# Longer stretches for the letters of a scheduling string: PIECE from 10000 to 16000, and a string made anew

## The chip, the cores and the metric

The kernel runs on one core of one Trainium2 chip. The metric is device time in microseconds (us) of one execution, and less is better. Each kernel is executed several times. The kernel before takes 689.98 us (median of 3 runs, 689.96 to 690.01).

## What is computed

There are 2048 tokens with 640 features. They are normalised (layernorm without weights). Two branches read the result `xn`, and the output is the input plus both of them. The first is attention with 32 query heads of 20 features that share one key head and one value head. The second is a feed-forward network 640 -> 1728 -> 640 with silu between.

```python
xn = layernorm(x)                                  # 2048 x 640
q = (xn @ wq) in 32 heads of 20;  k = xn @ wk;  v = xn @ wv
p = softmax(q @ k^T / sqrt(20))                    # 32 x 2048 x 2048
attn = (p @ v, heads side by side) @ wo
ffn = silu(xn @ w1) @ w2
out = x + attn + ffn
```

The softmax needs 32 x 2048 x 2048, some 134 million, exponentials, and these set the scale of the kernel.

## The kernel before, in words

**Tiling.** Queries are cut into 4 blocks of 512, heads into 8 groups of 4, keys into 16 tiles of 128. A *head tile* is one head, one key tile and one query block: a matmul with 32 contracted rows (L1078) that writes 128 x 512 scores into one PSUM bank. Four heads lie in the four row groups of TensorE's array, so up to four such matmuls run side by side. There are 4 x 8 x 16 x 4 = 2048 head tiles, in 32 groups (a query block and four heads) of 64.

**Two ways to an exponential.** The first is ScalarE (ACT): `make_s_act` (L1126) issues an operation named S for two or three head tiles into neighbouring banks, and one ACTIVATE with Exp (L1166) turns 128 x 1024 or 128 x 1536 scores into bf16. The second is an approximation in integer arithmetic: VectorE (DVE) adds a bias to one head tile and writes int16 (L1409, `p1`). When the four heads of a key tile are there, two copies with other shifts are made, one on GpSimd (POOL, L1448) and one on DVE or POOL (L1453, L1448), and the sum of the three, weighted, stands for the exponential. `dve_items` claims key tiles for this way, from the end of a group.

**Products with the values.** For each key tile of a group, four matmuls of 32 columns (L1201) add exp(scores) times v into one bank, U: one pass (PV) for a tile of ACT, three passes (PVd) for a tile of DVE, one for each shifted copy. At the end of a group U is copied out, divided by the sums (a POOL multiplication, L860, after a round of small DMAs) and packed for the output product.

**Other work of TensorE (PE).** Beside these come jobs: the query projections (`q`), the hidden layer (`h`, tanh on ACT at L773), the output tiles of the first three query blocks (`out`), and for the last block `y`: eight half tiles (128 x 320), each a chain of 14 to 17 passes at L447. A few of these passes are cut in row groups (L454, `row`) and laid beside a set of S matmuls that leaves a row group free. At the very end, for the last group alone, stand `sum` (L999), `spread` (L1017) and `fin` (L447): they divide by the last group's sums on PE, and add its product with wo to the y tiles. DVE then evicts five banks (L967) and the last stores go out.

**What sets the order.** All of this is one program that `build` works out in Python before anything runs. It keeps a clock for each engine with costs written into the file, and commits one operation after another. On PE, `step_pe` (L1842) collects candidates of the kinds S, PV, PVd, DVE head tile, row slice and job, and takes the first ready one in an order of preference. When nothing is ready and the gap it reckons is over 250 ns (120 ns after a pass of 32-column matmuls), it may put in a `fill`, a matmul on zeros (L1725). How it prefers is governed by some thirty parameters (BASE, L105): how far ahead of ACT an S may be, how long a job may hold back an S, how many batches may be open, and so on. A letter of the string PLAN names a small set of replacements for these (RULES, L106). Letter n holds while the planner's PE clock lies between n x PIECE and (n+1) x PIECE nanoseconds; behind the string's end the letter is `a`, which replaces nothing.

```python
while not finished():
    if sc.t["pe"] >= piece * PIECE:
        ru.__dict__.update(BASE)
        ru.__dict__.update(RULES[rule(piece)])
        piece += 1
```

Each engine then executes its own list strictly in that order. Waits between engines are semaphores that `emit` derives from what each operation reads and writes. So the string decides nothing but the order of the five lists and which operations share an instruction: how many head tiles one Exp takes, whether a shifted copy is on DVE or POOL, where fills stand, how many passes are cut in rows. The number of head tiles on ACT and on DVE can change too, since key tiles are claimed as the planner goes.

Of the kernel before, what the change touches and what calls it, by code (L numbers as in the profile page):

```python
# [81 lines left out]
POOL_J = (2,)  # L82
SWITCH = {"s": 97.0, "p": 98.0, "f": 98.0}
SPRIO = 0.5
PIECE = 10000.0
STEPS = 1
YC = (0, 0, 3, 3)
EARLY = 1
# [17 lines left out]
RULES = dict(a={}, b=dict(keep=0.0), c=dict(lagp=3), d=dict(lagp=5), e=dict(lagp=0), f=dict(patience=200.0), g=dict(dwant=0.0),  # L106
             h=dict(zcap=4), i=dict(zcap=3), j=dict(homes=0), k=dict(leadmax=-1.0, lead=-1.0), l=dict(lead=0.08, leadmax=0.1),
             m=dict(need=740.0), n=dict(hold=0.0), o=dict(stay=640.0), p=dict(open=1), q=dict(slack=560.0), r=dict(hungry=1000.0), s=dict(claim=9), t=dict(open=3), u=dict(claim=4), v=dict(want=2), w=dict(slack=850.0), x=dict(hold2=4), y=dict(bnd=0), z=dict(pj=-1e9), A=dict(rows=0), B=dict(rows=2, rowmin=2), C=dict(pj=2000.0), D=dict(openlag=3), E=dict(pj=8000.0), F=dict(hold2=3), G=dict(rows=1), H=dict(half=0), I=dict(half=3), J=dict(stay=560.0), K=dict(stay=720.0), P=dict(need=560.0), Q=dict(hold=120.0), L=dict(uopen=3), M=dict(uopen=4), N=dict(uopen=5), O=dict(uopen=0))
PLAN = "acbgxnoQpQJvpnaQodtxzpvEoQJBJoaodpJqQaDqJovpkBrnvxBxQJBfaaooHoatano"


def rule(n):
    return PLAN[n] if n < len(PLAN) else "a"
PACE = 1.0
# [214 lines left out]
def build(nc, A_x, A_wq, A_wk, A_wv, A_wo, B_x, B_w1, B_w2, out, stack):  # L329
# [1648 lines left out]
    def finished():  # L1978
        return (att["pgroup"] >= NGR and not pro and not misc and not misc_front and cur_job[0] is None
                and all(not sc.pools[e] for e in sc.ENG))  # L1980
# [3 lines left out]
# [3 lines that stand above are left out]
# [187 lines left out]
```

## Time and profile before

| what | value |
|---|---|
| median of 3 runs | 689.98 us |
| the profiled execution, whole | 690.16 us |
| its span, first to last instruction | 688.3 us |
| what lies around the span | 1.9 us |
| VectorE (DVE) busy | 591.3 us, 86% of the span |
| GpSimd (POOL) busy | 581.7 us, 85% |
| granted TensorE clock | 1.00 throughout |

The profile is one execution as the hardware recorded it. An engine is busy while at least one instruction of its own runs. Instructions of one engine overlap: the next begins before the last has left the pipeline. So the mean duration of an instruction is longer than the time by which it holds up its successor, and where a sum is wanted one takes the distance between starts. The ends of matmuls are modelled. "Idle before" is the time in which an engine ran nothing, and the releaser is the instruction whose end let it go on. The chain is followed back from the last instruction: at each step to what released it, or to the instruction before it on its engine.

### The profile page before, as it was taken

Reading aid. Unit: us, or ns where it says so; the run is one execution under the profiler, and the core shown is the slowest. Engines: PE = TensorE matmul, PEld = TensorE weight load, DVE = VectorE, ACT = ScalarE, POOL = GpSimd, SP = SyncE. Lnnn points to the kernel's source line nnn. Section 1 sums busy time; section 2 is a strip of 40 time slices with the busy share of each in tenths; the row PEclk is TensorE's granted clock in tenths of the full one; section 3 lists DMA queues with packets and bytes.
Section 4 is the critical chain, followed back from the end, with each engine's and each line's share of the span. In section 5 each row is a group of like instructions: output and inputs, shape, how many; then the busy total and the mean of one; then the engine's idle time right before and its main releaser. Section 6 shows DMA issues by size and latency. Waiting matters only on the chain.

```text
span 688.3 us, 22511 instructions
## 1 busy us (share of the span) xinstructions
PE 675.7 (98%) x9821; PEld 232.2 (34%) x9821; DVE 591.3 (86%) x1017; ACT 666.4 (97%) x728; POOL 581.7 (85%) x349
## 2 busy tenths in 40 slices
PE   8999999999999999999999999999999999999998
PEld 6432222222333333322323333332233333333345
DVE  7899988999989878798898897889999898987953
ACT  6999999999999999999999999999999999999992
POOL 6658899898988998899898889888889987879990
PEclk9999999999999999999999999999999999999999
DMA  8643220222221222422022222132222221223201
GB/s 226 190 160 42 19 23 14 35 34 25 23 29 12 32 38 29 72 36 30 9 22 30 29 31 33 26 37 61 31 22 20 21 27 23 32 20 70 23 7 41
DMA packets 34241, 28.97 MB, mean 42 GB/s; under 512 B 15486, under 2 KB 29662, under 8 KB 34142
## 3 DMA queue, kind: packets, MB, share of 16 engines
q1 hardware_dynamic: 33854, 27.20, 25.8%
q8 instruction: 77, 1.26, 0.8%
q10 hardware_dynamic: 288, 0.33, 0.1%
q14 instruction: 22, 0.18, 0.1%
HBM read 11.09 MB, written 2.62 MB: 20 GB/s over the span
## 4 chain that ended last, share of the span: by engine, by line
ACT 52%; PE 42%; DVE 3%; POOL 1%; DMA 0%; issue 0%; DVEq 0%; ACTq 0%
ACT sbt L1166 48%; PE psall L1201 14%; PE psall L1078 14%; PE psall L447 13%; ACT sbt L773 3%; DVE sbt L1409 2%; POOL sbt L1448 1%; PE psall L595 1%; PE psall L621 1%; DVE sbt L1453 0%; DMA sbt<-in_A_x_dram 0%; PE psall L999 0%; PE psall L1017 0%; ACT sbt L554 0%; DVE sbt L565 0%
## 5 line engine op out<-in xcount | busy, mean ns | idle before, releaser
L1166 ACT ACTIVATE sbt<-psall 128x1024 bf16<-128x1024 f32 (+1 forms) x656 | 640.0, 1138 | 3.2 <-PE psall L1078 3.0
L1448 POOL TENSOR_SCALAR sbt<-sbt 128x2048 int16<-128x2048 int16 x273 | 518.6, 1900 | 72.5 <-PE psall L1201 15.3
L1409 DVE TENSOR_SCALAR sbt<-psall 128x512 int16<-128x512 f32 x676 | 440.1, 685 | 63.1 <-PE psall L1078 58.0
L1078 PE MATMUL psall<-sbt 32*128 32x512 bf16 x2048 | 268.3, 384 | 3.3 <-ACT sbt L1166 2.0
L1201 PE MATMUL psall<-sbt 128*32 128x512 bf16 x3400 | 264.7, 384 | 1.9 <-POOL sbt L1448 0.6
L447 PE MATMUL psall<-sbt 128*32 128x320 bf16 (+2 forms) x3772 | 225.9, 332 | 2.1 <-DVE sbt L776 0.7
L1078 PEld LDWEIGHTS psall<-sbt 32*128 32x128 bf16 x2048 | 71.8, 91 | 236.9 <-ACT sbt L1166 174.1
L447 PEld LDWEIGHTS psall<-sbt 128*32 128x32 bf16 x3772 | 80.4, 95 | 85.5 <-issue 45.4
L1201 PEld LDWEIGHTS psall<-sbt 128*32 128x32 bf16 x3400 | 68.8, 94 | 115.5 <-issue 71.9
L1453 DVE TENSOR_SCALAR sbt<-sbt 128x2048 int16<-128x2048 int16 x65 | 47.6, 750 | 0.0
L860 POOL TENSOR_TENSOR sbt<-sbt 128x512 bf16<-128x512 f32 x30 | 38.3, 1277 | 4.9 <-DVE sbt L1453 2.7
L776 DVE SCALAR_TENSOR_TENSOR sbt<-sbt,psall 128x512 bf16<-128x512 bf16 x52 | 35.5, 682 | 3.8 <-ACT sbt L773 1.8
L773 ACT ACTIVATE sbt<-psall 128x512 bf16<-128x512 f32 x52 | 34.9, 671 | 0.2 <-PE psall L447 0.2
L454 PE MATMUL psall<-sbt 32*128 32x320 bf16 (+1 forms) x78 | 24.4, 313 | 0.0
L1250 DVE COPY sbt<-psall 128x512 f32<-128x512 f32 x31 | 21.2, 683 | 0.9 <-PE psall L1201 0.8
L919 DVE SCALAR_TENSOR_TENSOR sbt<-psall,sbt 128x320 f32<-128x320 f32 x8 | 3.9, 491 | 12.2 <-PE psall L447 7.0
L903 DVE SCALAR_TENSOR_TENSOR sbt<-psall,sbt 128x320 bf16<-128x320 f32 x24 | 11.6, 482 | 3.1 <-PE psall L447 1.7
L693 DVE TENSOR_SCALAR sbt<-psall 128x512 bf16<-128x512 f32 x20 | 13.5, 676 | 0.0
L572 POOL TENSOR_TENSOR sbt<-sbt 128x2 f32<-128x2 f32 x8 | 5.7, 710 | 8.5 <-DVE sbt L570 8.2
L1725 PE MATMUL psall<-sbt 128*32 128x256 bf16 (+1 forms) x188 | 11.1, 375 | 1.2 <-DVE sbt L487 1.2
L585 POOL TENSOR_SCALAR sbt<-sbt 128x640 bf16<-128x640 bf16 x12 | 10.4, 878 | 1.5 <-DVE sbt L577 1.5
L563 DVE BATCH_NORM_STATS2 sbt<-sbt 128x6 f32<-128x320 bf16 x14 | 6.6, 472 | 2.0 <-DMA sbt<-in_A_x_dram 2.0
(64 smaller groups left out, 118.3 us busy)
## 6 DMA issues: line engine op xcount, KB each, us to landing
sbt<-sbt SPq DMA_DIRECT2D x120, 64.0 KB, 3.8
sbt<-in_A_x_dram SPq DMA_DIRECT2D x28, 160.0 KB, 3.9
sbt<-sbt SPq DMA_DIRECT2D x213, 20.0 KB
out_dram<-sbt SPq DMA_DIRECT2D x14, 160.0 KB, 2.2
sbt<-in_B_w_dram SPq DMA_DIRECT2D x1, 2160.0 KB, 11.5
sbt<-in_B_w_dram SPq DMA_DIRECT2D x1, 2080.0 KB, 8.2
sbt<-sbt SPq DMA_DIRECT2D x75, 8.0 KB
sbt<-in_A_wq_dram SPq DMA_DIRECT2D x1, 800.0 KB, 6.7
```

The source lines that it names most:

```text
L447: ins = pe.matmul(ps[j * SLOT:(j + 1) * SLOT, b * BANK + off:b * BANK + off + n], w[:, j * SLOT:(j + 1) * SLOT], x, start=start, stop=stop ...
L454: return pe.matmul(ps[0:w.shape[-1], b * BANK:b * BANK + n], w[k], x[k], start=start, stop=stop, tile_position=(r * SLOT, 0))
L773: t = Op("act", lambda a: a.activation(t_buf[0:rows, ts, :], bk(job.bank, 0, QW, rows=rows), AF.Tanh, scale=0.5), t_act(512), ACT_END, pre ...
L776: u = Op("dve", lambda v: v.scalar_tensor_tensor(out=hT[par][0:rows, fk, :], in0=t_buf[0:rows, ts, :], scalar=1.0, in1=bk(job.bank, 0, QW, ...
L860: nm = pool(lambda e: e.tensor_tensor(oU[:, us, :], U_sb[:, us, :], Rrep, ALU.mult), 1356.0, POOL_END, pre=[uc] + lc + pack_op.get(divmod( ...
L1078: return pe.matmul(bk(b), kT_rep[i * SLOT:(i + 1) * SLOT, kt * P:(kt + 1) * P], qT[i * SLOT:(i + 1) * SLOT, g % NQ, :], start=True, stop=T ...
L1166: return a.activation(Ebuf[:, es * QW:es * QW + w], ps[:, buf[0] * BANK:buf[0] * BANK + w], AF.Exp, scale=ESCALE)
L1201: ins = pe.matmul(ps[i * SLOT:(i + 1) * SLOT, ub * BANK:ub * BANK + QW], lhsT, rhs, start=(first and k < HG), stop=(last and k >= len(lst) ...
L1250: return v.tensor_copy(U_sb[:, us, :], bk(ub))
L1409: p1 = Op("dve", lambda v: v.tensor_scalar(z16[:, i * QW:(i + 1) * QW], bk(job.bank), ZBIAS, 0.0, ALU.add, ALU.max), t_dve(QW) + 2.0, DVE_ ...
L1448: op = pool(lambda v, t=t, j=j, zin=zin: v.tensor_scalar(t.bitcast(I16), zin, float(SHIFT[j]), 1.0, ALU.add, ALU.mult), POOL_SHIFT, POOL_E ...
L1453: op = dve(lambda v, t=t, j=j, zin=zin: v.tensor_scalar_add(t.bitcast(I16), zin, float(SHIFT[j])), t_dve(N, 4), prio=SPRIO - 0.01 * j, **args)
```

## The change

Two constants are replaced. PIECE becomes 16000, so that a letter holds for 16000 ns of the planner's clock and not for 10000. The string becomes one of 42 letters where it had 67, and the two have only their first letter in common. The parameters that the letters stand for, all costs and every function are untouched.

```diff
-PIECE = 10000.0
+PIECE = 16000.0
...
-PLAN = "acbgxnoQpQJvpnaQodtxzpvEoQJBJoaodpJqQaDqJovpkBrnvxBxQJBfaaooHoatano"
+PLAN = "apQdxxjnrnvQBCfnDoQLoQDQyDGoEJutBtEonoPzrg"
```

## The prediction

> **What bounds the kernel now.** I read the page first. Span, busy shares and the chain:
>
> ```profile
> span 688.3 us, 22511 instructions
> PE 675.7 (98%) x9821; PEld 232.2 (34%) x9821; DVE 591.3 (86%) x1017; ACT 666.4 (97%) x728; POOL 581.7 (85%) x349
> ACT 52%; PE 42%; DVE 3%; POOL 1%; DMA 0%; issue 0%; DVEq 0%; ACTq 0%
> ```
>
> PE and ACT are both nearly always busy, and the chain changes between them, so the page alone does not say which of the two sets the end. [...]
>
> So next I took the groups of ACT by form, its waits, its chain and its timeline, to see how full its stream is when one counts distances between starts:
>
> ```profile
> L1166 ACT ACTIVATE sbt<-psall 128x1024 bf16<-128x1024 f32 x594 | 563.5, 1100 | 2.6 <-PE psall L1078 2.5
> L1166 ACT ACTIVATE sbt<-psall 128x1536 bf16<-128x1536 f32 x61 | 89.7, 1512 | 0.6 <-PE psall L1078 0.6
> L773 ACT ACTIVATE sbt<-psall 128x512 bf16<-128x512 f32 x52 | 34.9, 671 | 0.2 <-PE psall L447 0.2
> L744 ACT ACTIVATE sbt<-psall 128x512 bf16<-128x512 f32 x2 | 1.3, 639 | 0.0
> L1166 ACT ACTIVATE sbt<-psall 128x512 bf16<-128x512 f32 x1 | 0.7, 700 | 0.0
> ```
> ```profile
> ACT sbt L1166 <- PE psall L1078: 3.0, 7, 0.6
> ```
> ```profile
> 304.43 0.49 ACT sbt L773
> 304.93 3.67 ACT sbt L1166 x4
> ```
> ```profile
> 13.64 1.92 ACT L1166 ACTIVATE sbt<-psall 128x1024 bf16<-128x1024 f32 x2
> ...
> 34.96 1.94 ACT L1166 ACTIVATE sbt<-psall 128x1024 bf16<-128x1024 f32 x2 [0.16 <-PE psall L1078]
> ...
> 37.26 11.98 ACT L1166 ACTIVATE sbt<-psall 128x1024 bf16<-128x1024 f32 x12
> ```
> ```profile
> 514.13 1.44 ACT L1166 ACTIVATE sbt<-psall 128x1536 bf16<-128x1536 f32 x1
> 515.46 0.60 ACT L773 ACTIVATE sbt<-psall 128x512 bf16<-128x512 f32 x1
> ```
> ```profile
> L1166 ACT ACTIVATE sbt<-psall x656: 700/1096/1647, 13.6 to 674.4; 128x1024 bf16<-128x1024 f32 x151, 128x1536 bf16<-128x1536 f32 x13
> ```
>
> A double Exp (two head tiles) holds ACT for 3.67 / 4 = 0.918 us, a triple for 515.46 - 514.13 = 1.33 us, a tanh for 0.49 us. From 37.26, where the dense part begins, to 674.4, where the last Exp starts, are 637.1 us. 22 doubles lie ahead of it (in five groups of which the first and the last are quoted). So it holds 594 - 22 = 572 doubles, 61 triples and 54 tanhs: 572 x 0.918 + 61 x 1.33 + 54 x 0.49 = 525.1 + 81.1 + 26.5 = 632.7 us. ACT therefore waits only 637.1 - 632.7 = **4.4 us** in the whole body. In the body ACT is the bound, and an order can win there at most these 4.4 us.
>
> After the last Exp it is another engine's turn. The timeline of the end:
>
> ```profile
> 673.65 0.38 PE L1078 MATMUL psall<-sbt 32*128 32x512 bf16 x1
> 673.66 0.30 PE L454 MATMUL psall<-sbt 32*128 32x320 bf16 x1
> 673.97 1.41 PE L447 MATMUL psall<-sbt 128*32 128x320 bf16 x36
> 675.20 0.39 PE L1201 MATMUL psall<-sbt 128*32 128x512 bf16 x4
> 675.42 2.62 PE L447 MATMUL psall<-sbt 128*32 128x320 bf16 x72
> 677.97 1.05 PE L999 MATMUL psall<-sbt 128*128 128x4 f32 x8
> 678.95 1.08 PE L1017 MATMUL psall<-sbt 128*32 128x128 f32 x32
> 679.85 5.11 PE L447 MATMUL psall<-sbt 128*32 128x128 bf16 x144
> 684.35 1.34 DVE L967 SCALAR_TENSOR_TENSOR sbt<-psall,sbt 128x512 bf16<-128x512 f32 x2 [0.30 <-PE psall L447]
> ```
>
> From the last S at 673.65 on, PE's groups follow without a gap up to 679.85 + 5.11 = 684.96; then come the last evictions and stores, to 688.3. So the last 14.6 us are **PE's list behind the last S**, whatever ACT does. The end is thus: the start of the last Exp, less the lead of its S (674.4 - 673.65 = 0.75), plus what PE has behind that S.
>
> **The change part by part.** The two programs' lists can be counted, and their order compared, without running them. The first 215 operations of PE and the first 45 of ACT are the same, so the start up to the dense part stays. The work is nearly the same too: 676 head tiles on DVE in both, 1372 on ACT, the same passes of PV and PVd (850), 273 shifted copies on POOL against 274.
>
> *ACT.* 590 doubles and 64 triples, no single, against 594, 61 and one. The last Exp is now a double, where it was the single. Ahead of the last Exp stand 589 doubles and 64 triples against 594 and 61: -5 x 0.918 + 3 x 1.33 = **-0.6 us**. Tanhs are the same.
>
> *PE behind the last S.* This is the one place where the lists differ by much. Before, as the rows show: 9 y passes, one PV, 18 y passes, sum, spread, fin. Behind the last S of the changed list stand 6 PV passes, 1 y, 1 PV, 3 y, 1 PV, 13 y, sum, spread, 17 y and the same fin: 8 passes of 512 columns where there was 1, and 34 y passes where there were 27. A y pass takes (677.97 - 675.42) / 18 = 0.14 us. For a pass of 512 columns:
>
> ```profile
> 301.34 0.62 PE L447 MATMUL psall<-sbt 128*32 128x512 bf16 x8
> 301.89 0.39 PE L1078 MATMUL psall<-sbt 32*128 32x512 bf16 x3
> ...
> 304.82 0.83 PE L1201 MATMUL psall<-sbt 128*32 128x512 bf16 x12
> 305.48 0.60 PE L447 MATMUL psall<-sbt 128*32 128x512 bf16 x8
> ```
>
> Three passes take 305.48 - 304.82 = 0.66, one 0.22 us. So 7 x 0.22 + 7 x 0.14 = 1.54 + 0.98 = **+2.5 us**, and nothing hides it: PE's groups there already follow without a gap. The last PVd waits for a POOL copy of 1.90 us (row below), and behind it on PE stands all the rest; 13 y passes (1.8 us) cover the way from it to sum, which takes U's copies on ACT; 17 y passes and the first fin cover spread's multiplication.
>
> ```profile
> L1448 POOL TENSOR_SCALAR sbt<-sbt 128x2048 int16<-128x2048 int16 x273 | 518.6, 1900 | 72.5 <-PE psall L1201 15.3
> ```
>
> *The lead of the last S.* Before 0.75 us. In the changed list its banks are free long before, and one S and four passes stand just ahead of it, 0.33 + 4 x 0.22 + 0.11 = 1.3 us, the time of the triple that ACT runs meanwhile; so it keeps the lead of the S before it. That one needs the banks of the Exp two back. I take 0.75 again: 0. Bounds: not under 0.39, the matmul itself in the row of 301.89 (+0.4), and not over 1.33, the triple (-0.6).
>
> *PE in the body.* 1318 changes between matmuls of 32 contracted rows and those of 128, where there were 1329. Two passes and a change back take 301.89 - 301.34 = 0.55, so a change costs 0.55 - 0.44 = 0.11 us: -11 x 0.11 = -1.2 us. Ten fewer row slices come back as 3 more full passes, +0.4. Together -0.8, and the 2.5 us moved behind the last S are gone from the body as well: PE has 3.3 us less to do there. Seven more fills (54 for 47; 5 of 512 columns, 2 of 256: 1.3 us) stand where the planner saw PE idle. As ACT is the bound, all this counts only in how late an S comes. I counted, from S to S, where PE's list holds more work than ACT's Exps of that stretch: before 238 of 636 stretches, by over 0.2 us 48; changed 249 and 64. So there is less work, but a little more unevenly laid. The bounds are a gain of the whole 4.4 us and a loss of as much; I take 0, between the two signs.
>
> **Sum.** -0.6 + 2.5 + 0 + 0 = +1.9 us. Against the profiled execution, whose span of 688.3 with 1.9 around it makes 690.16, this gives 692.1; that execution is 0.2 over the median of 689.98, so the forecast of the median is **691.9 us**, +0.28%. A measurement of this kernel can tell about 0.2%, or 1.4 us, from no change.
>
> **The rivals.**
>
> *Fewer waits in the body (faster).* PE's 3.3 us less could let S come in time: the place is the 4.4 us of waits from 37 to 674. Each us less is a us won. It turns the sign when waits fall by more than 1.9, to under 2.5, and is faster by over 0.2% only from 1.1 on down. With nearly all gone: 691.9 - 3.5 = 688.4. For it speaks the smaller load; against it the unevenness, and that a wait of 4.4 us in 656 Exps is already little. Chance 0.12.
>
> *PE's whole work sets the end.* If the chain's 42% of PE are the truth, where the 2.5 us stand does not matter, only the total of -0.8: 689.2. The busy row of PE speaks for it; against it, that ACT's starts leave only 4.4 us. Chance 0.18. [...]
>
> *More waits in the body.* If waits grow as the uneven stretches do, 64 to 48, they become 4.4 x 64 / 48 = 5.9 us: +1.5, 693.4. Chance 0.18.
>
> *POOL holds up the last PVd.* The last five shifted copies of the changed list stand on POOL in one row, 9.5 us, and one of them waits for a PV of the batch before it. Were POOL one copy late, all of PE's rest moves: up to +1.9, 693.8. POOL's idle time before copies (72.5 us in the row) speaks against it. Chance 0.05.
>
> **How the numbers follow.** The forecast has 0.47, with a range of its own from 690.6 to 693.2 by the lead's bounds and about 1 us of waits; about a quarter of it, 0.12, lies under 691.4, within 0.2%. Slower by over 0.2%: 0.35 + 0.18 + 0.05 = 0.58. Within: 0.12 + 0.18 = 0.30. Faster: 0.12. The range from 688.7 to 694.0 takes in the second rival and both of the slower ones, and leaves out nearly all of the first and what lies beyond two bad cases at once.
>
> **What would show it.** Right: the last Exp starts within 1 us of 673.8 in the changed trace; PE runs without a gap from the last S for some 13.8 us (11.3 before); the span is about 690.2. Wrong: a last Exp before 672.5 (first rival) or behind 675 (third); a gap of PE ahead of the last L1201 row, with POOL as releaser (fourth); ACT waiting long in the body while PE has no gap (second).

## The result and the profile after

The changed kernel takes 691.41 us (median of 16 executions, 690.62 to 693.30). The kernel before takes 689.98 us beside it (16 executions, 689.68 to 690.82). The ratio is 1.0023, with a 95% interval of 1.0016 to 1.0030: **1.4 us slower**. The profiled execution of the changed kernel took 692.16 us, with a span of 690.4 us and a mean granted clock of 0.998.

The first lines of its page, and its chain by engine:

```profile
span 690.4 us, 22564 instructions
...
PE 678.3 (98%) x9851; PEld 234.6 (34%) x9851; DVE 592.1 (86%) x1014; ACT 665.9 (96%) x726; POOL 583.1 (84%) x350
...
ACT 56%; PE 38%; DVE 3%; POOL 1%; issue 1%; DMA 0%; DVEq 0%; POOLq 0%; ACTq 0%
```

As before, busy times don't tell what holds the end: PE's rose by 2.6 us and ACT's fell by 0.5. So the next views are those of ACT: its groups by form, its waits, and the line of the Exps with the first and last start.

```profile
L1166 ACT ACTIVATE sbt<-psall 128x1024 bf16<-128x1024 f32 x590 | 563.4, 1108 | 3.1 <-PE psall L1078 2.9
L1166 ACT ACTIVATE sbt<-psall 128x1536 bf16<-128x1536 f32 x64 | 95.7, 1511 | 0.5 <-PE psall L1078 0.4
```
```profile
ACT sbt L1166 <- PE psall L1078: 3.3, 9, 0.5
```
```profile
L1166 ACT ACTIVATE sbt<-psall x654: 1003/1110/1652, 13.6 to 673.6; 128x1024 bf16<-128x1024 f32 x149, 128x1536 bf16<-128x1536 f32 x15
```

The last Exp starts at 673.6, where it was 674.4. The counts are those of the list: 590 doubles and 64 triples. The end on PE is the timeline from the last S on. (A row of it has start and length in us, engine, line and operation, output and input, shapes, and count. Brackets give the idle time ahead of it and its releaser.)

```profile
673.16 0.39 PE L1078 MATMUL psall<-sbt 32*128 32x512 bf16 x2
673.48 1.48 PE L1201 MATMUL psall<-sbt 128*32 128x512 bf16 x24
674.79 0.31 PE L447 MATMUL psall<-sbt 128*32 128x320 bf16 x4
...
675.65 0.40 PE L1201 MATMUL psall<-sbt 128*32 128x512 bf16 x4
675.88 1.94 PE L447 MATMUL psall<-sbt 128*32 128x320 bf16 x52
677.75 1.05 PE L999 MATMUL psall<-sbt 128*128 128x4 f32 x8
678.74 1.08 PE L1017 MATMUL psall<-sbt 128*32 128x128 f32 x32
679.63 7.42 PE L447 MATMUL psall<-sbt 128*32 128x320 bf16 x212
```

No row has a gap ahead of it. From the last S to the end of PE's last group are 679.63 + 7.42 - 673.16 = 13.9 us, where it was 11.3, and to the end of the span 690.4 - 673.16 = 17.2, where it was 14.6. So the profiled executions differ by 2.1 us like this: the last Exp starts 0.8 earlier, its S leads it by 0.48 and not by 0.75 (+0.3), and what follows the last S is 2.6 longer.

**The 16 executions are not of one kind.** Six have a mean granted clock of 0.998, the others 1.000:

```
clock 0.998: 692.16 692.18 692.22 692.24 692.29 693.30
clock 1.000: 690.62 690.70 690.77 690.77 690.81 690.82 690.84 691.23 691.59 692.22
```

The median of the six is 692.23, that of the ten 690.81. The profiled one is of the six. Its clock was at half for one stretch of 3.41 us, at 360 us; in a span of 690 that makes a mean of 0.998. (For the other five the mean alone is known, not the place.) Of 70 executions of the kernel before, taken beside the experiments, none has a mean under 0.999. The table by stretches there (time, PE, PEld, DVE, ACT and POOL busy with counts, granted clock, DMA share, GB/s):

```profile
352.95:356.36 3.41, 3.41 (x48) 0.96 (x44) 3.10 (x6) 3.41 (x5) 3.33 (x2) 1.00 0.07 17
356.36:359.77 3.41, 2.54 (x23) 0.68 (x19) 3.23 (x6) 3.41 (x5) 3.25 (x3) 1.00 0.07 14
359.77:363.18 3.41, 3.41 (x29) 0.59 (x25) 2.62 (x5) 2.75 (x3) 3.25 (x3) 0.50 0.00 0
```

In the stretch ahead of it PE ran only 23 matmuls where it had 48, and was idle for a quarter of the time; then came the half clock, and ACT, full until then, lost 0.66 us in that row. PE's timeline over the thin stretch shows why it was thin, and ACT's timeline what followed:

```profile
357.30 0.79 PE L1078 MATMUL psall<-sbt 32*128 32x512 bf16 x4
358.70 0.57 PE L1078 MATMUL psall<-sbt 32*128 32x512 bf16 x4 [0.62 <-ACT sbt L1166]
359.49 0.40 PE L1201 MATMUL psall<-sbt 128*32 128x512 bf16 x4 [0.21 <-DVE sbt L1409]
359.82 0.61 PE L1078 MATMUL psall<-sbt 32*128 32x512 bf16 x2
```
```profile
357.56 3.93 ACT L1166 ACTIVATE sbt<-psall 128x1024 bf16<-128x1024 f32 x4
361.98 1.02 ACT L1166 ACTIVATE sbt<-psall 128x1024 bf16<-128x1024 f32 x1 [0.49 <-PE psall L1078]
363.43 4.85 ACT L1166 ACTIVATE sbt<-psall 128x1024 bf16<-128x1024 f32 x5 [0.42 <-PE psall L1078]
```

PE has nothing it may do: the next S needs banks that an Exp still reads, the next PV a head tile that DVE makes. At half clock the S of 359.82 takes 0.61 us and not 0.39, and two Exps wait for theirs.

**Theories for the experiments.** Theory 1 is the prediction's sum: work behind the last S counts in full, work of PE in the body does not, ACT's stream counts. Rival A: PE's whole work counts, wherever it stands. Rival B: the half clock, not the tail, makes the difference. Open was also what the waits in the body depend on.

### The profile page after: what moved, and what is told of

The parts are those of the page before. It is cut to its first block, busy times and chain, and to the rows that moved or that the text cites. A ratio compares the mean times of both kernels' runs of the same rounds, so it can differ in the third digit from the quotient of the medians.

```text
span 690.4 us, 22564 instructions
## 1 busy us (share of the span) xinstructions
PE 678.3 (98%) x9851; PEld 234.6 (34%) x9851; DVE 592.1 (86%) x1014; ACT 665.9 (96%) x726; POOL 583.1 (84%) x350
## 4 chain that ended last, share of the span: by engine, by line
ACT 56%; PE 38%; DVE 3%; POOL 1%; issue 1%; DMA 0%; DVEq 0%; POOLq 0%; ACTq 0%
ACT sbt L1166 52%; PE psall L1201 12%; PE psall L1078 12%; PE psall L447 11%; ACT sbt L773 3%; DVE sbt L1409 1%; POOL sbt L1448 1%; PE psall L595 1%; PE psall L621 1%; DVE sbt L776 0%; DMA sbt<-in_A_x_dram 0%; PE psall L1017 0%; PE psall L999 0%; ACT sbt L554 0%; DVE sbt L565 0%
## 5 line engine op out<-in xcount | busy, mean ns | idle before, releaser
L1201 PE MATMUL psall<-sbt 128*32 128x512 bf16 x3400 | 264.5, 385 | 1.6 <-DVE sbt L1409 0.6
L447 PEld LDWEIGHTS psall<-sbt 128*32 128x32 bf16 x3784 | 82.1, 95 | 85.9 <-issue 45.4
L1201 PEld LDWEIGHTS psall<-sbt 128*32 128x32 bf16 x3400 | 70.5, 94 | 115.7 <-issue 72.4
L454 PE MATMUL psall<-sbt 32*128 32x320 bf16 (+1 forms) x68 | 21.3, 314 | 0.0
L595 PE MATMUL psall<-sbt 128*128 128x128 bf16 x80 | 7.0, 220 | 1.4 <-DVE sbt L588 1.4
```

What stands on the lines that cost most here:

```text
L447: ins = pe.matmul(ps[j * SLOT:(j + 1) * SLOT, b * BANK + off:b * BANK + off + n], w[:, j * SLOT:(j + 1) * SLOT], x, start=start, stop=stop ...
L454: return pe.matmul(ps[0:w.shape[-1], b * BANK:b * BANK + n], w[k], x[k], start=start, stop=stop, tile_position=(r * SLOT, 0))
L1201: ins = pe.matmul(ps[i * SLOT:(i + 1) * SLOT, ub * BANK:ub * BANK + QW], lhsT, rhs, start=(first and k < HG), stop=(last and k >= len(lst) ...
```

## The experiments

Each edit stands at the end of `build`, unless another place is shown. Times of the kernel before are those taken beside each experiment. The bracket behind a ratio is its 95% interval.

**awake: the thin stretch filled.** Three passes on zeros are put ahead of the head-tile matmul that PE waits to issue at 358.

```diff
 # of the changed kernel
+late = next(o for o in sc.order["pe"] if o.name == "sd16_12_3")
+def awake(pe, base=late.fn, b=late.job.bank):
+    for _ in range(3):
+        for i in range(HG):
+            pe.matmul(ps[i * SLOT:(i + 1) * SLOT, b * BANK:(b + 1) * BANK], zero_t[:, 0:SLOT],
+                      zero_t[:, 0:QW], start=True, stop=True, tile_position=(0, i * SLOT))
+    return base(pe)
+late.fn = awake
```

> The changed kernel with three passes of zero matmuls (12 matmuls, 0.65 us) put on PE into the idle stretch at 357.7 to 358.7, in a bank that is overwritten right behind them; nothing else differs and the output is the same. Theory 1: what lifts the changed kernel from about 690.8 to 692.2 in part of its executions is the half clock of 3.4 us at 360, and that comes from PE having been idle too long just before. Then every execution lies between 690.5 and 691.0, the granted clock is 1.00 in all windows, and the last Exp starts about 1.5 us earlier than 673.6, near 672.1. Rival: the scatter has another source (DMA, POOL), and some 6 of 16 executions still lie at 692.2 or above with or without the passes.

Measured: 691.21 us (690.63 to 692.12, 11 executions), ratio 1.0018 (1.0010 to 1.0027). The mean clock is 0.999 or 1.000 in all 11, so none shows the half-clock stretch; at a rate of 6 in 16 the chance of that is 0.625^11 = 0.6%. Its profiled execution took 690.73. The same two stretches of time, PE's filling, and ACT:

```profile
356.36:359.77 3.41, 3.25 (x35) 0.91 (x31) 3.23 (x6) 3.41 (x5) 3.25 (x3) 1.00 0.07 14
359.77:363.18 3.41, 3.41 (x48) 0.95 (x44) 3.41 (x8) 3.41 (x5) 3.25 (x3) 1.00 0.00 0
```
```profile
357.98 0.83 PE L2019 MATMUL psall<-sbt 128*32 128x512 bf16 x12
```
```profile
357.53 11.16 ACT L1166 ACTIVATE sbt<-psall 128x1024 bf16<-128x1024 f32 x12
```
```profile
L1166 ACT ACTIVATE sbt<-psall x654: 1002/1113/1653, 13.6 to 672.2; 128x1024 bf16<-128x1024 f32 x149, 128x1536 bf16<-128x1536 f32 x15
```

With 0.7 us more work PE kept its clock, ACT ran through this stretch without a wait, and the last Exp came at 672.2 and not 673.6. Set Exp by Exp against this trace, the starts of the changed kernel agree within 0.05 us up to 359. Then they fall behind by 0.18, 0.61, 0.54 and 0.13 us at four neighbouring Exps, and stay 1.42 to 1.44 behind to the end. So the half clock costs 1.4 us, and the thin stretch brings it on. But six of the 11 executions still lie between 691.21 and 692.12, at full clock. The median fell by only 0.2 us, from 691.41: the rest of the scatter has another source.

**tail_cut: 15 of the 17 y passes between `spread` and `fin` left out.**

```diff
 # of the changed kernel
+for op in [o for o in sc.order["pe"] if o.name == "y3_3_1"][1:-1]:
+    op.fn = lambda pe: None
```

> The changed kernel without 15 of the 17 y passes that stand between spread and fin behind the last S (they are left out: the last half tile lacks 15 of its 17 partial products). Theory 1: the end is PE's list behind the last S, so each pass costs its 0.142 us: 2.1 us less from the last S to the end, 13.9 -> 11.8 us of PE and 17.2 -> 15.1 us in all, and the time falls by 2.1 to about 689.3 (688.7 in executions without a half clock). Rival: the passes lie beside the division of the last group (sum, spread, multiplication, eviction), and the time falls by under 0.5.

Measured: 690.69 us (689.37 to 692.99, 10 executions), ratio 1.0010 (1.0000 to 1.0021). The profiled execution has the half clock at 360 too (last Exp at 674.0), so the tail is compared from the last S on. It stands at 673.52 and the span ends at 689.2: 15.7 us, 1.5 less than the 17.2. The end of PE's list:

```profile
679.10 1.08 PE L1017 MATMUL psall<-sbt 128*32 128x128 f32 x32
679.99 0.46 PE L447 MATMUL psall<-sbt 128*32 128x320 bf16 x8
680.72 5.11 PE L447 MATMUL psall<-sbt 128*32 128x128 bf16 x144 [0.27 <-DVE sbt L1026]
```

The passes left out are 15 x 0.14 = 2.1 us, and 1.5 come off. Most of the missing 0.6 is in these rows: the first `fin` now starts 0.73 us behind the start of the two passes that are left, where back to back it would be 0.28, and it waits for the multiplication on DVE (L1026), which the full 17 passes cover. So three or four of the 15 lie beside that multiplication, and the rest counts. Six of the ten executions have a mean clock of 0.997 or 0.998 (690.65 to 692.99), four 0.999 or more (689.37 to 690.09). The median of these four is 689.6, 1.2 us under that of the changed kernel at full clock. The list has the same thin stretch as the changed kernel (busy for 2.52 of 3.40 us in the trace), so beside awake's none of 11 stand six of 10 without the zero passes.

**before_nofill: no fill in the dense part.**

```diff
 # of the kernel before
+first = next(k for k, o in enumerate(sc.order["pe"]) if o.name == "S38")
+for op in sc.order["pe"][first:]:
+    if op.name == "fill":
+        op.fn = lambda pe: None
```

> The kernel before without its 11 fills in the dense part (zero matmuls; the output is the same). Theory 1: fills keep PE's clock up: without them at least one stretch of 3.4 us at half clock appears, most likely near 108 or 315 us where PE's list is thinnest, and the time goes up by 1 to 1.5 us for each, 691 to 692.5. Rival: fills stand in idle time and are of no effect either way: 690.0 within 0.3, clock 1.00 throughout.

Measured: 690.08 us (689.74 to 691.28, 10 executions), ratio 1.0003 (0.9994 to 1.0012). In its profiled execution the last Exp starts at 674.5, and the mean clock is 1.000. So the eleven fills do nothing for the median of that list. One of the ten executions, that of 691.28, has a mean clock of 0.998, as none of 70 of the kernel before has. That the fills keep the clock up there is not shown by one execution.

**before_light: 3.5 us of PE's work left out of the body.**

```diff
 # of the kernel before
+names = [f"h{q}_{f}" for q in range(QC) for f in range(FC - 1)]
+for n in names[6::3]:
+    op = [o for o in sc.order["pe"] if o.name == n][2]
+    op.fn = lambda pe: None
```

> The kernel before without 16 passes of 512 columns in its dense part (the third of the five passes of every third h job is left out, so those parts of the hidden layer lack a fifth of their sum): 16 x 0.22 = 3.5 us less work for PE between 60 and 600 us, the order of all else unchanged. Theory 1: ACT's waits in the body follow PE's load, as the changed kernel with its 3.3 us less shows: the last Exp starts 1 to 2 us before 674.4 and the time falls to 688.0 to 689.0. Rival: waits come from the local order, not from the load, and the time stays within 0.4 of 690.0.

Measured: 690.02 us (689.74 to 690.29, 10 executions), ratio 1.0000 (0.9990 to 1.0009). The line of its Exps:

```profile
L1166 ACT ACTIVATE sbt<-psall x656: 700/1102/1654, 13.6 to 674.4; 128x1024 bf16<-128x1024 f32 x151, 128x1536 bf16<-128x1536 f32 x13
```

The last Exp starts at 674.4, as before. 3.5 us less of PE, the size of what the change took from the body, changes nothing, so for these passes rival A is false. They stood between 77 and 532 us, 11 of the 16 ahead of 353. None stood in the last 140 us ahead of the last S, and for that stretch the run says nothing.

**before_letter_t: letter 64 of the string before, `a`, becomes `t`** (three jobs may be open at once), to see whether y passes can leave the tail.

```diff
-PLAN = "acbgxnoQpQJvpnaQodtxzpvEoQJBJoaodpJqQaDqJovpkBrnvxBxQJBfaaooHoatano"
+PLAN = "acbgxnoQpQJvpnaQodtxzpvEoQJBJoaodpJqQaDqJovpkBrnvxBxQJBfaaooHoattno"
```

> The kernel before with one letter of its string changed (the one for 640 to 650 us, a to t). PE's list is the same up to S631 (3281 of 3491 operations), the sum of ACT's stream ahead of the last Exp differs by 0.1 us, and behind the last S stand no y pass any more, 10 fin passes, two PV, sum, spread and 17 fin passes, where there were 27 y, one PV, sum, spread and 36 fin. Theory 1: the end is what stands behind the last S. With 27 + 9 passes of 0.14 us gone the list is short enough that the way of the last group sets the end: last Exp and PV (2.7 us to U's copies), sum and spread (2.0), 17 passes or multiplication and evictions (3.8), stores (2.6): about 11.4 us from the last S, against 14.6; time 686.4 to 687.6. Rival: the y work only moves ahead of the last S and delays ACT's stream by as much, and the time stays within 0.5 of 690.0.

Measured: 691.33 us (691.05 to 691.92, 11 executions) against 689.85, ratio 1.0021 (1.0012 to 1.0030). From the last S at 678.24 to the end at 689.3 are 11.1 us, 3.5 less than before. But the last Exp starts at 679.3, 4.9 later. ACT's timeline, and PE's at the same time:

```profile
654.30 6.88 ACT L1166 ACTIVATE sbt<-psall 128x1536 bf16<-128x1536 f32 x6
666.81 13.17 ACT L1166 ACTIVATE sbt<-psall 128x1536 bf16<-128x1536 f32 x11 [5.63 <-PE psall L1078]
```
```profile
659.12 0.40 PE L1078 MATMUL psall<-sbt 32*128 32x512 bf16 x4
659.44 1.26 PE L1201 MATMUL psall<-sbt 128*32 128x512 bf16 x20
660.53 1.94 PE L447 MATMUL psall<-sbt 128*32 128x320 bf16 x52
662.62 0.40 PE L1201 MATMUL psall<-sbt 128*32 128x512 bf16 x4
662.84 3.16 PE L447 MATMUL psall<-sbt 128*32 128x320 bf16 x88
665.83 0.60 PE L1201 MATMUL psall<-sbt 128*32 128x512 bf16 x8
666.37 0.40 PE L1078 MATMUL psall<-sbt 32*128 32x512 bf16 x4
```

Between the S of 659.12 and that of 666.37 PE ran 35 y passes, and ACT was idle for 5.6 us. The y work left the tail, and it was put in one block ahead of an S that ACT needed. The end came out as theory 1 has it (11.1 us for 11.4), but theory 1 took the last Exp to stay where it was. The loss of 1.5 us is also more than the 0.5 of the rival.

**letter_Q_awake: the same aim from the changed kernel,** with the zero passes of awake, and letter 40 of its string, `r`, made `Q`.

```diff
-PLAN = "apQdxxjnrnvQBCfnDoQLoQDQyDGoEJutBtEonoPzrg"
+PLAN = "apQdxxjnrnvQBCfnDoQLoQDQyDGoEJutBtEonoPzQg"
```

> The changed kernel with one letter of its string changed (the one for 640 to 656 us, P or what stands there, to Q), and with the three zero passes of the experiment awake. Behind the last S stand no y pass, 2 PV, 11 fin, sum, spread, 15 fin; ACT's stream ahead of the last Exp is 2.2 us longer by its doubles and triples (672 head tiles on DVE for 676). Theory 1: last Exp 2.2 later than awake's 672.2, so 674.4, and 11.4 us from the last S to the end as in the kernel before with another letter: 687.0, from 686.5 to 688.5. Rival: as there, 690.7 or more.

Measured: 693.12 us (693.00 to 694.38, 5 executions), ratio 1.0050 (1.0037 to 1.0062). It is the same picture: 11.1 us from the last S (680.23) to the end (691.3), and one hole on ACT, while PE ran almost only y passes from 660.98 to 666.5:

```profile
667.98 14.03 ACT L1166 ACTIVATE sbt<-psall 128x1536 bf16<-128x1536 f32 x11 [6.77 <-PE psall L1078]
```

**string_only and piece_only: one of the two constants alone.**

```diff
 # string_only: the new string
 PIECE = 10000.0
 # piece_only: the old string
 PIECE = 16000.0
```

> The new string with PIECE at 10000 as before: each letter now holds for 10000 ns of the planner's clock, and behind 420 us no letter holds. Counted from the lists: 640 head tiles on DVE for 676, so ACT's stream ahead of the last Exp is 14.1 us longer; PE's list behind the last S has no y pass and is 1.1 us shorter. Theory 1 (ACT's stream plus the end behind the last S): 690.0 + 14.1 - 1.1 = 703.0, from 701 to 706. Rival: the two constants work apart from each other and the string alone carries the change: 691.4 within 1.

> The old string with PIECE at 16000: its letters reach 42 of 67 and each stands elsewhere in the order than before. Counted: 620 head tiles on DVE for 676, ACT's stream ahead of the last Exp 21.4 us longer; behind the last S no y pass, PE's list 3.6 us shorter, which the way of the last group limits to some 3. Theory 1: 690.0 + 21.4 - 3 = 708.4, from 706 to 712. Rival: PIECE alone is harmless, 690 to 692.

Measured: 713.85 us (711.98 and 715.72), ratio 1.0347 (1.0320 to 1.0374), and 717.70 us (716.41 and 718.99), ratio 1.0403 (1.0383 to 1.0423). Expected were 703 and 708.4. ACT's groups by form, of string_only and then of piece_only:

```profile
L1166 ACT ACTIVATE sbt<-psall 128x1024 bf16<-128x1024 f32 x548 | 527.2, 1106 | 3.9 <-PE psall L1078 3.6
L1166 ACT ACTIVATE sbt<-psall 128x1536 bf16<-128x1536 f32 x104 | 157.2, 1537 | 6.2 <-PE psall L1078 6.0
```
```profile
L1166 ACT ACTIVATE sbt<-psall 128x1024 bf16<-128x1024 f32 x513 | 499.1, 1107 | 3.8 <-PE psall L1078 3.6
L1166 ACT ACTIVATE sbt<-psall 128x1536 bf16<-128x1536 f32 x134 | 201.2, 1551 | 5.5 <-PE psall L1078 5.5
```

Against the 594 doubles and 61 triples before, ACT's stream is longer by -46 x 0.918 + 43 x 1.33 = 15.0 us in the one and by -81 x 0.918 + 73 x 1.33 = 22.7 us in the other: some 60% and 80% of the 24.0 and 27.9 us lost. (Ahead of the last Exp it is 14.1 and 21.4.) So head tiles moved from DVE to ACT, and most of the rest is waits, for which I had counted nothing: the idle time ahead of Exps is 10.1 and 9.3 us, where it was 3.2. Here too there are stretches at half clock, at 535.4 in string_only and at 350.3 and, twice as long, at 555.1 in piece_only, each behind a thin one (that ahead of 555.1 has PE busy for 2.18 of 3.40 us). In string_only and piece_only, for the first two:

```profile
532.00:535.41 3.41, 1.43 (x16) 0.43 (x16) 2.05 (x4) 3.41 (x4) 3.25 (x3) 1.00 0.09 23
535.41:538.82 3.41, 3.16 (x40) 1.02 (x36) 1.98 (x3) 3.41 (x3) 3.33 (x2) 0.50 0.02 6
```
```profile
346.90:350.30 3.40, 1.80 (x22) 0.40 (x14) 2.77 (x6) 3.40 (x5) 3.24 (x3) 1.00 0.02 6
350.30:353.70 3.40, 3.33 (x27) 0.69 (x27) 1.13 (x2) 2.91 (x3) 3.24 (x3) 0.50 0.07 18
```

The two constants belong together; neither part alone can be set against the whole.

**before_tail_add: work added behind the last S.** 18 passes of 320 columns on zeros stand in the middle of the last y tile.

```diff
 # of the kernel before
+late = [o for o in sc.order["pe"] if o.name == "y3_3_1"][8]
+def more(pe, base=late.fn, job=late.job):
+    for _ in range(18):
+        for i in range(HG):
+            pe.matmul(ps[i * SLOT:(i + 1) * SLOT, job.bank * BANK:job.bank * BANK + HALF], zero_t[:, 0:SLOT],
+                      zero_t[:, 0:HALF], start=False, stop=False, tile_position=(0, i * SLOT))
+    return base(pe)
+late.fn = more
```

> The kernel before with 18 passes of zero matmuls of 320 columns (18 x 0.142 = 2.55 us) added to PE's list behind the last S, in the middle of the last y job, whose bank they leave as it is; the output is the same. Theory 1: the step that the prediction priced at +2.5 us is a plain 1:1 cost, since PE's list behind the last S sets the end: +2.5 on the median, 692.4, PE's list 13.9 us instead of 11.3, last Exp still at 674.4. Rival: part of it lies beside the way of the last group (as 0.56 us of the passes left out in tail_cut did), and the cost is 2.0 or less.

Measured: 692.14 us (692.01 to 692.20, 6 executions) against 689.70, ratio 1.0034 (1.0022 to 1.0047): +2.44 us. PE's timeline:

```profile
676.14 2.62 PE L2019 MATMUL psall<-sbt 128*32 128x320 bf16 x72
678.58 1.40 PE L447 MATMUL psall<-sbt 128*32 128x320 bf16 x36
```

The added passes hold PE for 678.58 - 676.14 = 2.44 us, and from the last S (673.15) to the end of PE's list are 13.75 us for 11.31, the same 2.44 more. Work behind the last S costs one to one. The last Exp, expected at 674.4, starts at 673.9 in this execution: the wait of 0.30 us that ACT has at 654.95 in the profile of the kernel before is not in it.

**awake_b and awake_c: the kernel awake, one execution each,** for a profile of the longer kind at full clock.

> The experiment awake once more, for another execution's trace: 6 of its 11 executions were at 691.2 to 692.1, the other 5 at 690.6 to 690.9, and the profiled one was of the lower kind. Theory 1: what is left of the scatter is a wait of ACT of 0.4 to 1.4 us in the body at one place or a few, which a trace of the upper kind shows beside that of the lower. Rival: it is spread over the whole span, or lies in the start or the last stores.

> A third execution of the experiment awake for its trace, with the same question as awake_b. Theory 1: if it is of the upper kind, a wait of 0.4 to 1.4 us of ACT at the same place as there. Rival: spread over the span, or in the start or the last stores.

Measured: 690.60 and 690.68 us. Both are of the shorter kind, so they tell nothing of the other. That question stays open.

**before_body_add: the same 18 passes in the body,** one in each of 18 output tiles between 220 and 614 us.

```diff
 # of the kernel before
+for q in range(QC - 1):
+    for t in range(QTP):
+        for hf in range(2):
+            if (t, hf) in ((0, 0), (2, 1)):
+                continue
+            late = [o for o in sc.order["pe"] if o.name == f"out{q}_{t}_{hf}"][8]
...
+            late.fn = more        # one pass on zeros, then the pass that stood there
```

> The kernel before with the same amount of zero matmuls as in before_tail_add (18 passes of 320 columns, 2.55 us), but one each in 18 of the 24 out jobs, between 240 and 640 us, in the jobs' own banks; the output is the same. Theory 1: it is the place that decides, since ACT's stream is the bound there: the time rises by no more than 0.5 us, and the last Exp starts within 0.5 of 674.4. Rival: PE's whole work sets the end, and the time rises by 2 to 2.5 us as it did behind the last S.

Measured: 691.36 us (691.29 to 691.69, 10 executions) against 689.66, ratio 1.0025 (1.0016 to 1.0035): +1.70 us. Neither expectation holds. The line of the Exps, and ACT's waits:

```profile
L1166 ACT ACTIVATE sbt<-psall x656: 702/1072/1641, 13.6 to 675.7; 128x1024 bf16<-128x1024 f32 x151, 128x1536 bf16<-128x1536 f32 x13
```
```profile
ACT sbt L1166 <- PE psall L1078: 2.7, 6, 0.6
```

By 650 us the Exps start 1.7 us later than in the kernel before, and the last one 1.3 later, since the wait of 0.30 us at 654.95 is not in this execution either. Yet the view of waits shows no more than before (2.7 where it was 3.0, without that one wait). The loss is made of small steps between the starts of neighbouring Exps, at most 0.13 us each. Behind each of the 18 passes they come to between 0.01 and 0.14 us; the latter is the time of a whole pass. Successive Exps overlap (1.1 us long, some 0.9 apart), so a delay that small leaves no idle time to see; only the starts show it. So these 18 passes cost two thirds of themselves, where the 16 that before_light left out, at other places, gave nothing.

## Why the prediction came out as it did

**Slower by 1.4 us, with 1.9 forecast: the mechanism of the end holds, one term, the body, was mis-sized, and that the two numbers lie so close is in part luck.** In the profiled executions the terms are:

| term | forecast | measured |
|---|---|---|
| ACT's stream | -0.6 | -0.6 |
| PE behind the last S | +2.5 | +2.6 |
| lead of the last S | 0 (+0.4 to -0.6) | +0.3 |
| waits in the body, full clock | 0 | -1.5 |
| the half clock at 360 us | not priced | +1.4 in 6 of 16 executions |

*ACT's stream.* The counts came out as the lists have them, and 37.25 to 673.6 is 636.35 us. By the prediction's own holds (567 doubles, 64 triples and 54 tanhs ahead of the last Exp) 632.1 of it are work.

*PE behind the last S.* 13.9 us without a gap, for the 13.8 given as a sign. before_tail_add shows the same price from the other side: 2.44 us of passes, +2.44 us.

*The lead.* 0.48 us, near the bound of 0.39 and not at the 0.75 that I took. It does keep the lead of the S before it, as was argued: in the trace that one starts at 671.86 and its Exp at 672.30, a lead of 0.44. What failed is that 0.75 was taken for that lead.

*The body: this step failed.* "I take 0, between the two signs." It looks right in the profiled execution, where 4.2 us of waits stand for the 4.4 before, but two things cancel in it. In awake, whose list is the same but for three passes, the last Exp starts at 672.2 and the waits are 672.2 - 37.23 - 632.1 = 2.9. So the changed order has 1.5 us fewer waits at full clock, and in 6 of 16 executions a half-clock stretch takes 1.4 of them back. The count of uneven stretches, 64 to 48, which I used as the argument for more waits, pointed the wrong way at full clock. And where PE's list is thin I looked only for how late an S would come and not at the clock. "Seven more fills" were seen as a mark that the planner saw PE idle, and then priced by their work alone.

*The size of the waits.* The 4.4 us themselves are misread. The hold of a double, 0.918 us, came from one row of four Exps. These rows of the kernel before give (347.94 - 343.42) / 5 = 0.904:

```profile
343.42 4.81 ACT L1166 ACTIVATE sbt<-psall 128x1024 bf16<-128x1024 f32 x5
347.94 0.78 ACT L773 ACTIVATE sbt<-psall 128x512 bf16<-128x512 f32 x1
```

0.904 is also the median of all 572 distances between the start of a double and that of the next instruction on ACT; for a tanh it is 0.478. So 572 x 0.904 + 61 x 1.33 + 54 x 0.478 = 624.0 us are work, and ACT waits 13.1 us in the kernel before, 12.9 in the changed one and 11.5 in awake. The differences stay as they were (-1.6 and +1.4), but "at most these 4.4 us" is too low: an order can win at most 13.1 us there, of which 10.9 are waits under 0.25 us each.

*Nor is ACT the bound in the whole body.* In the kernel before, the chain as the profile follows it runs on ACT for 97% of the time from 37 to 360 us, but on PE for 74% from 360 to 543 and for 91% from 543 to the last Exp. In awake it is on PE for 95% from 540 on. So the two pace by turns. Behind 450 us the waits went from 5.8 to 4.0 us (the kernel before and awake), ahead of it from 7.3 to 7.5. All that was won lies where the chain of the kernel before runs mostly on PE.

*By the sums.* At full clock: -0.6 + 2.6 + 0.3 - 1.5 = +0.8, and the ten executions at full clock have a median of 690.81, +0.8 against 689.98. With the half clock it is +2.2, and the six have +2.2 (692.23). So rival B, the half clock alone, does not make the whole difference: at full clock +0.8 remain. The median of all 16 falls between these two heaps, so its +1.4 is the time of neither, and its nearness to the +1.9 of the forecast rests on how often the half clock came.

**The rivals.** *Fewer waits in the body* was right in its place and in most of its size: 1.5 us, short of the 1.9 where the sign turns. Its reason, the smaller load of PE, is open: before_light took 3.5 us of PE's work away and won nothing, but none of it behind 532 us, where about half of the waits were won and where the chain runs on PE. Whether the load or the order there won them, no run showed. *PE's whole work sets the end* is false as it was put: before_light again; and added passes cost all of their time behind the last S, two thirds in the body. But those two thirds, and the chain, say that PE's work does count in part of the body. *More waits* is false as a whole (4.2 us, not 5.9), though 1.4 of them came by a way that it did not name. *POOL holds up the last PVd* did not come about: no gap stands ahead of PE's last L1201 row.

**What no run settled.** Three executions of the changed kernel and six of awake lie between 691.2 and 692.3 at full clock, and none of these was profiled. And no version was found that beats the kernel before. Shorter tails were had twice, by a letter, at the price of a hole on ACT that was longer than the gain.

## What to carry to other kernels

When one engine paces a program and another finishes it, count the two apart: the pacing engine's list to its last instruction, and the finishing engine's list behind it. Here 18 passes put in behind the last S cost their whole time, 2.44 us. What a pass gives or costs in the body has to be measured where it stands: 16 passes left out gave nothing, 18 put in elsewhere cost two thirds of their time. Moving work out of the tail did not help, two times, where it came to stand in one block ahead of what the pacing engine needed. And take an instruction's hold from many starts, not from one row: 0.014 us too much, 572 times, hid 8 of 13 us of waits. Where an order leaves TensorE as thin for some 3 us as here (busy for 2.54 of 3.41), look at the granted clock in more than one execution: here the price, 1.4 us, came in 6 of 16.

## What the hardware showed that was not expected

The clock went to half though TensorE had not been idle throughout the row ahead of it. By the profile it was busy there for 2.54 of 3.41 us in the changed kernel (longest gap 0.62 us), 1.43 in string_only, and 1.80 of 3.40 in piece_only. The kernel before has a stretch of 2.51 of 3.40 us busy with 29 matmuls and not 23, and in its trace the clock stays at 1.00 there and in the 3.40 us behind it. So busy time alone doesn't tell the two apart:

```profile
108.30:111.70 3.40, 2.51 (x29) 0.67 (x25) 2.38 (x5) 3.40 (x5) 3.24 (x3) 1.00 0.00 0
```

What it is in the thin stretch that brings the clock down, and why one list has it in 6 of 16 executions and not in all, no run showed. awake shows that with three passes in the thin stretch (busy for 3.25 of 3.41 us, not 2.54) the clock stays at 1.00 behind it.

The stretch of 3.41 us at half clock cost 1.4 us of the end, 41% of its length: the Exps behind it stay late by as much to the end.
